# Attention planned by TensorE tiling, with the Newton step of the inverse roots on GpSimd

## The chip, the cores and the metric

The kernel runs on one core of a Trainium2 chip. The metric is the device time in microseconds (us) of one execution. The engines of the core run side by side and are synchronised by semaphores: TensorE (matrix products, in the profile PE, and PEld for its weight loads), VectorE (DVE), ScalarE (ACT), GpSimd (POOL), and SyncE (SP), from whose queue all DMA transfers are issued. SBUF is the working memory of 128 partitions, PSUM the memory of eight banks that TensorE writes to.

## The reference

Three parts follow one another: attention with normalised queries and keys, a soft mixture of experts, and a gated product.

```python
# q, k, v: batch 4, heads 12, seq 448, head_dim 64
def rmsnorm(x, g):
    rms = np.sqrt(np.mean(x * x, axis=-1, keepdims=True) + 1e-06)
    return x / rms * g
q_n, k_n = (rmsnorm(q, g_q), rmsnorm(k, g_k))
scores = scale * np.matmul(q_n, k_n.transpose(0, 1, 3, 2))
scores = scores - np.max(scores, axis=-1, keepdims=True)
attn = np.exp(scores)
attn = attn / (np.sum(attn, axis=-1, keepdims=True) + 1e-09)
attn_out = np.matmul(attn, v)
...
# x: 1792 x 768 from attn_out; phi: 768 x 32; w1, w2: 8 experts, 768 x 1024 and 1024 x 768
logits = x @ phi
# softmax over tokens picks slot inputs, each expert: relu(slots @ w1[e]) @ w2[e],
# softmax over slots mixes the expert outputs back to tokens
...
a = x @ w_a          # 768 x 1536
b = x @ w_b
return a * b @ w_out # 1536 x 768
```

## The kernel before, in words

Everything that the change touches lies in attention, the first of three stages in the program (some 340 us of the profiled execution). Attention works on 24 pairs of heads (`p`), each with two heads (`hd`) and four chunks of 112 rows (`c` for queries, `kc` for keys). For each pair the steps are:

- `LQ`, `LV`: loads of q, k and of v from DRAM (SP). Three pairs of q and k fit in SBUF (`qk`); the next load waits until `NM` has read an older one.
- `SQ`: squares of q (`i` = 0, GpSimd, except for the first three pairs) and of k (`i` = 1, ScalarE); `SS`: their sums over the head dimension (VectorE).
- `RT`, function `root`: the inverse roots on ScalarE as exp(-0.5 ln x), three instructions on 112 x 16 values. Two of them are the same exponential, one written to SBUF (`nt`) and one to PSUM.
- `NW`, function `newton`: one Newton step of the inverse roots, on VectorE, three instructions on 112 x 16 values. Its scratch is in PSUM, in the unused columns of the bank `psv` (`spare_ps`), whose other columns hold the value products `A`.
- `NM`: q and k times the roots (GpSimd; `i` = 0 on VectorE for two pairs). `T`: transposes on TensorE. `H` and `L`: each value is split into a high and a low part (ScalarE, VectorE); `Z`: six DMA transfers that stack these for the scores.
- `X`, function `peak`: products of the high parts, two matmuls side by side, one for each head, on 64 rows of the array each. `MX`: their maxima on VectorE. One PSUM buffer (`x`) serves all `X`. `R` and `RW`: the maxima as rows.
- `S`, function `score`: two matmuls for each chunk and head, on the full array (lines 346 and 347). `E`: the exponential (ScalarE).
- `AD`: additions of exponentials over the chunks (GpSimd). `A`, function `av`: the products with v, four matmul records, each head on 64 columns of the array. `D`, function `den`: the sums, likewise on 64 columns. `LN`, `EX`, `N1`, `N2`, `F`: reciprocals and the output of the pair.

After each six pairs the operations of the experts' softmaxes for that batch are mixed in (`moe_ops`): logits `lm` and `ln` and token sums `ac` are matmuls with 32 columns each, so on column strips.

The order of the instructions on each engine is made when the program is built, by a planner. `op` enters an operation with its engine, a cost, a due time (`prio`: the pair's number times `T0` = 11.5 plus the offset of its kind in `OFF`), its dependencies, and buffers that it takes and gives. `plan` then plays the operations through: each engine that is free takes, of the operations that are ready and have room, the one with the earliest due time. The instructions are written out in the order of the planned starts, and each engine runs its own in that order, waiting wherever its data isn't there. Where TensorE has a planned gap at the start or at the end of attention, matmuls on the identity fill it (`warm`), as do `W0` of them at the very start, in the bank `psv`.

Eight loads of expert weights, 1.5 MB each, are issued among the pairs' transfers; the other weights follow as the buffers of attention come free.

Of the kernel before, what the change touches and what calls it, by code (L numbers as in the profile page):

```python
# [32 lines left out]
def kernel(  # L33
# [20 lines left out]
    NC = 4  # L54
# [19 lines left out]
    W0 = 22  # L74
    SQ_ACT = (1,)
    NPT, T0, MSTEP, WU0, WUS, MF, = 5, 11.5, 3.2, 4, 2, 13
    OFF = dict(LQ=-29.0, LV=-12.6, SQ=14.4, SS=32.6, RT=21.7, NW=-22.2, NM=9.2, T=-16.7, H=-11.9, L=9.7, Z=5.9, X=-9.0, MX=-2.3, R=0.4, RW=13.2, S=5.4, E=8.3, AD=-29.5, A=19.0, D=7.6, LN=-51.5, EX=-19.7, N1=-7.9, N2=7.7, F=-53.1)
    MO = (-0.1, -0.9, 21.5, 82.1)
# [127 lines left out]
    with ExitStack() as c1:  # L206
# [52 lines left out]
        def root(p):  # L259
            t = sm.tile([P, 16], F32, tag="nt", name="nt", bufs=2)  # L260
            act.activation(out=t, in_=ssq_t[p].rearrange("p a c -> p (a c)"), func=AF.Ln, bias=ssq_eps[0:P])
            act.activation(out=spare_ps(0, 16), in_=t, func=AF.Exp, scale=-0.5)  # L262
            act.activation(out=t, in_=t, func=AF.Exp, scale=-0.5)
            nt_t[p] = t

        def newton(p, s):
            t, x, y = spare_ps(16, 16), ssq_t[p].rearrange("p a c -> p (a c)"), nt_t[p]
            if s == 0:
                dve.scalar_tensor_tensor(out=t, in0=spare_ps(0, 16), scalar=-0.5, in1=y, op0=ALU.mult, op1=ALU.mult)
            elif s == 1:  # L270
                dve.scalar_tensor_tensor(out=t, in0=x, scalar=D * 1e-6, in1=t, op0=ALU.add, op1=ALU.mult)
            else:
                r = rinv_t[p] = sm.tile([P, 2, 8], F32, tag="rinv", name=f"rinv{p}", bufs=3)
                dve.scalar_tensor_tensor(
                    out=r.rearrange("p a c -> p (a c)"), in0=t, scalar=1.5, in1=y, op0=ALU.add, op1=ALU.mult
                )
# [126 lines left out]
        def op(eng, cost, prio, name, fn, deps=(), take=(), give=()):  # L403
            names[name] = len(ops)
            ops.append((eng, cost, prio, fn, [names[d] for d in deps], take, [(k, names[n]) for k, n in give]))
            return name
# [4 lines left out]
        def pair_ops(p):  # L411
# [15 lines left out]
            for s in range(3):  # L427
                op("DVE", 0.20, o("NW"), ("NW", p, s), lambda s=s: newton(p, s), [("NW", p, s - 1) if s else ("RT", p)])
# [216 lines left out]
        def start_up():  # L645
            ps = ps_of["w"] = bank
            warm(ps, W0)

# [682 lines left out]
```

## Time and profile before

| | |
|---|---|
| median of 3 runs | 591.88 us (587.56, 591.88, 592.78) |
| profiled execution | 587.84 us, span 586.1 us |
| mean granted TensorE clock | 0.981 |
| TensorE busy | 557.8 us (95%), 3564 matmuls |
| VectorE busy | 333.9 us (57%) |
| ScalarE busy | 319.1 us (54%) |
| GpSimd busy | 231.4 us (39%) |
| mean DMA rate | 229 GB/s, 427 GB/s between 370 and 480 us |

The span is the time from the first to the last instruction of one profiled execution. A busy share is an average over all three stages. Matmuls are pipelined and their ends are modelled, so consecutive ones overlap in the records; what one takes is read from its start to the start of the next.

### The profile page before, as it was taken

The numbers are of one execution on the slowest core, as the hardware profiler recorded it, in microseconds if no ns is written. First come the engines' busy times: TensorE is split into PE (matmuls) and PEld (weight loads), VectorE is DVE, ScalarE is ACT, GpSimd is POOL, SyncE is SP. The second block draws the span as 40 slices with busy tenths as digits, with TensorE's granted clock in tenths as the row PEclk, the third lists the DMA queues.
The fourth block names the chain that finished last, engine by engine and source line by source line (L and its number), as shares of the span: only waits on it lengthen the run. The fifth ranks groups of instructions, "written<-read, shape, count | busy, mean of one in ns | idle before, by whom it ended". The sixth has DMA issues, their size and how long they took to land.

```text
span 586.1 us, 9656 instructions
## 1 busy us (share of the span) xinstructions
PE 557.8 (95%) x3564; PEld 326.8 (56%) x3564; DVE 333.9 (57%) x556; ACT 319.1 (54%) x607; POOL 231.4 (39%) x167
## 2 busy tenths in 40 slices
PE   8799999999999899999999999898999999999997
PEld 8645444444444444443454455333675656689996
DVE  2778778677776467877656331122248788742211
ACT  4367767667666457666666531111279889432210
POOL 1288887567785356886654700011100000200000
PEclk9999999999999599999999998999999999999999
DMA  6598699969899378999684869999999991002332
GB/s 164 131 232 188 154 271 265 203 192 214 240 202 259 67 211 180 260 211 249 141 218 111 326 244 410 427 427 423 423 425 423 421 426 57 0 29 83 98 89 81
DMA packets 42622, 134.42 MB, mean 229 GB/s; under 512 B 5840, under 2 KB 31440, under 8 KB 36176
## 3 DMA queue, kind: packets, MB, share of 16 engines
q1 hardware_dynamic: 42576, 133.81, 74.7%
q8 instruction: 28, 0.46, 0.3%
q14 instruction: 18, 0.15, 0.1%
HBM read 95.26 MB, written 5.51 MB: 172 GB/s over the span
## 4 chain that ended last, share of the span: by engine, by line
PE 81%; DMA 7%; DVE 5%; ACT 4%; issue 1%; POOL 1%; SPq 1%; ACTq 0%; DVEq 0%; POOLq 0%
PE psv L365 12%; PE pss L346 8%; PE pss L347 6%; PE psx L324 5%; DMA z<-e 4%; PE psM L1046 4%; PE psh L805 4%; PE psS L829 4%; PE pso L1246 3%; PE pso L1248 3%; PE pso L1247 3%; PE psden L373 3%; PE pst L293 3%; PE psv L201 3%; DMA xw<-in_k_dram 3%; PE psL L201 2%
## 5 line engine op out<-in xcount | busy, mean ns | idle before, releaser
L352 ACT ACTIVATE pt<-pss 112x448 f32<-112x448 f32 x192 | 98.2, 541 | 49.8 <-PE pss L347 44.1
L329 DVE TENSOR_REDUCE nmx<-psx 112x2 f32<-112x896 f32 x96 | 104.5, 1088 | 31.2 <-PE psx L324 30.1
L357 POOL TENSOR_TENSOR sum<-sum,pt 112x896 f32<-112x896 f32 x48 | 100.6, 2096 | 13.2 <-ACT pt L352 11.2
L365 PE MATMUL psv<-pt,v 112*64 112x448 f32 x384 | 94.2, 572 | 2.8 <-ACT psv L262 2.5
L346 PE MATMUL pss<-z 128*112 128x448 f32 x192 | 83.0, 432 | 1.0 <-DMA z<-e 0.9
L347 PE MATMUL pss<-z 66*112 66x448 f32 x192 | 71.6, 373 | 0.6 <-DMA z<-e 0.6
L281 POOL TENSOR_TENSOR n<-xw,rinv 112x512 f32<-112x512 f32 x46 | 48.3, 1064 | 60.4 <-PE pst L293 30.2
L357 POOL TENSOR_TENSOR sum<-pt,pt 112x896 f32<-112x896 f32 x24 | 50.3, 2096 | 32.7 <-ACT pt L352 24.2
L346 PEld LDWEIGHTS pss<-z 128*112 128x112 f32 x192 | 34.0, 177 | 42.8 <-issue 20.3
L324 PE MATMUL psx<-e 64*112 64x448 f32 x192 | 44.2, 456 | 1.9 <-DVE nmx L329 1.6
L324 PEld LDWEIGHTS psx<-e 64*112 64x112 f32 x192 | 16.7, 170 | 48.4 <-DVE nmx L329 16.1
L1246 PE MATMUL pso<-Mh,t 128*128 128x384 f32 x112 | 37.9, 339 | 0.5 <-DVE Ml L1075 0.5
L1248 PE MATMUL pso<-Mh,t 128*128 128x384 f32 x112 | 37.9, 338 | 0.0
L1247 PE MATMUL pso<-Ml,t 128*128 128x384 f32 x112 | 37.8, 338 | 0.0
L365 PEld LDWEIGHTS psv<-pt,v 112*64 112x64 f32 x384 | 19.7, 137 | 31.5 <-issue 22.2
L1098 POOL TENSOR_TENSOR t<-CC,t 128x512 fp32r<-128x512 f32 x2 | 3.7, 1882 | 82.0 <-DVE G L1005 82.0
L347 PEld LDWEIGHTS pss<-z 66*112 66x112 f32 x192 | 34.4, 179 | 2.8 <-DMA z<-e 1.1
L1265 DVE COPY ot<-pso 128x384 f32<-128x384 f32 (+1 forms) x14 | 7.6, 544 | 49.7 <-PE pso L1250 49.7
L1046 PE MATMUL psM<-w,G 128*128 128x512 f32 x64 | 33.8, 610 | 0.8 <-DVE G L1009 0.8
L255 DVE TENSOR_REDUCE ssq<-sq 112x8 f32<-112x512 f32 x48 | 31.9, 677 | 4.3 <-POOL sq L250 3.2
L908 ACT ACTIVATE top<-wu_w,few 128x1536 f32<-128x1536 int8 x18 | 31.4, 1746 | 0.4 <-DVE xw L926 0.4
L926 DVE SCALAR_TENSOR_TENSOR xw<-wu_w,top 128x768 int32<-128x768 int32 x24 | 22.2, 954 | 15.7 <-ACT top L912 15.7
(186 smaller groups left out, 966.3 us busy)
## 6 DMA issues: line engine op xcount, KB each, us to landing
wu_w<-in_moe_w_dram SPq DMA_DIRECT2D x38, 1536.0 KB, 13.3
z<-e SPq DMA_DIRECT2D x48, 336.0 KB, 5.7
z<-e SPq DMA_DIRECT2D x48, 224.0 KB, 6.1
r<-in_moe_w_dram SPq DMA_DIRECT2D x7, 1536.0 KB, 9.9
xw<-in_moe_w_dram SPq DMA_DIRECT2D x4, 1536.0 KB, 13.5
xw<-in_q_dram SPq DMA_DIRECT2D x24, 224.0 KB, 5.4
xw<-in_k_dram SPq DMA_DIRECT2D x24, 224.0 KB, 5.4
v<-in_v_dram SPq DMA_DIRECT2D x24, 224.0 KB, 4.4
```

What stands on the lines that cost most here:

```text
L281: eng.tensor_tensor(out=n_t[p][:, i].rearrange("p c h d -> p h c d"), in0=qk_t[p][:, i].rearrange("p h (c d) -> p h c d", d=D), in1=rinv_t ...
L324: pe.matmul(ps[:, hd], et[r, QH, c * P:(c + 1) * P], et[r, KH, :], start=True, stop=True)
L329: dve.tensor_reduce(out=nm_t[p][:, c, :], in_=ps_of[p, "x"], axis=AX.X, op=ALU.max, negate=True)
L346: pe.matmul(ps, z[:, 1, c], z[:, 0, :], start=True, stop=False)
L347: pe.matmul(ps, z[0:66, 2, c], z[0:66, 3, :], start=False, stop=True)
L352: act.activation(out=pt_t[p, kc][:, hd, :], in_=ps_of.pop((p, kc, hd)), func=AF.Exp)
L357: pool.tensor_tensor(out=sum_t[p], in0=pt_t[p, 0] if kc == 1 else sum_t[p], in1=pt_t[p, kc], op=ALU.add)
L365: pe.matmul(av_t[p][hd * D:(hd + 1) * D, 0:S], v_t[p][:, hd, kc, :], pt_t[p, kc][:, hd, :], start=(kc == 0), stop=(kc == NC - 1),)
L1046: pe.matmul(o, G[:, r], W[:, c], start=st, stop=sp_)
L1246: pe.matmul(o, ch[:, m], Mh[:, m, c], start=(m == 0), stop=False)
L1247: pe.matmul(o, ch[:, m], Ml[:, m, c], start=False, stop=False)
L1248: pe.matmul(o, cl[:, m], Mh[:, m, c], start=False, stop=False)
```

## The change

The planner learns of the way in which a matmul tiles TensorE's array. Each operation gets a mode (`MODES`): 0 full array, 1 row halves (`X`), 2 column halves (`A`, `D`), 3 column strips (`lm`, `ln`, `ac`). On TensorE the planner adds `MW` = 18.97 to the due time of an operation whose mode differs from that of the one before, when it chooses, and `MSW` = 0.1 us to its cost, when it is taken. The other TensorE costs are changed, and all offsets in `OFF` and `MO`.

The Newton step moves from VectorE (three operations of the plan) to GpSimd (one operation, four instructions), all of whose operands lie in SBUF. The root writes both its results to SBUF; its third instruction squares the second one's result.

At the start, `W0` falls from 22 to 8 identity matmuls; ahead of them stand 16 pairs of 448-column matmuls on `zt[1]` (`WR`), tiled in row halves, into the buffer of `X`. The operation `ones` on ScalarE, which now also fills `zt[1]`, is planned ahead of it.

```diff
--- before.py
+++ after.py
@@ -71,11 +71,12 @@
     LW, LO, LG = 8, 4, 2
     XLAST = 5
     NU = 3076
-    W0 = 22
+    W0, WR = 8, 16
     SQ_ACT = (1,)
     NPT, T0, MSTEP, WU0, WUS, MF, = 5, 11.5, 3.2, 4, 2, 13
-    OFF = dict(LQ=-29.0, LV=-12.6, SQ=14.4, SS=32.6, RT=21.7, NW=-22.2, NM=9.2, T=-16.7, H=-11.9, L=9.7, Z=5.9, X=-9.0, MX=-2.3, R=0.4, RW=13.2, S=5.4, E=8.3, AD=-29.5, A=19.0, D=7.6, LN=-51.5, EX=-19.7, N1=-7.9, N2=7.7, F=-53.1)
-    MO = (-0.1, -0.9, 21.5, 82.1)
+    OFF = dict(LQ=-166.2, LV=33.1, SQ=261.0, SS=546.8, RT=249.0, NW=-272.3, NM=304.6, T=-12.7, H=222.0, L=-181.2, Z=-53.0, X=-22.7, MX=346.8, R=1.6, RW=16.9, S=10.7, E=21.9, AD=-243.9, A=25.1, D=-215.8, LN=-88.7, EX=-311.9, N1=-104.9, N2=245.2, F=3.0)
+    MODES, MSW, MW = {"X": 1, "A": 2, "D": 2, "lm": 3, "ln": 3, "ac": 3}, 0.1, 18.97
+    MO = (28.8, 9.4, 27.9, 225.6)
     WE = 7
     WN = 11
     WS = 3
@@ -257,23 +258,20 @@
             )
 
         def root(p):
-            t = sm.tile([P, 16], F32, tag="nt", name="nt", bufs=2)
-            act.activation(out=t, in_=ssq_t[p].rearrange("p a c -> p (a c)"), func=AF.Ln, bias=ssq_eps[0:P])
-            act.activation(out=spare_ps(0, 16), in_=t, func=AF.Exp, scale=-0.5)
-            act.activation(out=t, in_=t, func=AF.Exp, scale=-0.5)
+            t = sm.tile([P, 2, 16], F32, tag="nt", name="nt", bufs=2)
+            act.activation(out=t[:, 0], in_=ssq_t[p].rearrange("p a c -> p (a c)"), func=AF.Ln, bias=ssq_eps[0:P])
+            act.activation(out=t[:, 0], in_=t[:, 0], func=AF.Exp, scale=-0.5)
+            act.activation(out=t[:, 1], in_=t[:, 0], func=AF.Square)
             nt_t[p] = t
 
-        def newton(p, s):
-            t, x, y = spare_ps(16, 16), ssq_t[p].rearrange("p a c -> p (a c)"), nt_t[p]
-            if s == 0:
-                dve.scalar_tensor_tensor(out=t, in0=spare_ps(0, 16), scalar=-0.5, in1=y, op0=ALU.mult, op1=ALU.mult)
-            elif s == 1:
-                dve.scalar_tensor_tensor(out=t, in0=x, scalar=D * 1e-6, in1=t, op0=ALU.add, op1=ALU.mult)
-            else:
-                r = rinv_t[p] = sm.tile([P, 2, 8], F32, tag="rinv", name=f"rinv{p}", bufs=3)
-                dve.scalar_tensor_tensor(
-                    out=r.rearrange("p a c -> p (a c)"), in0=t, scalar=1.5, in1=y, op0=ALU.add, op1=ALU.mult
-                )
+        def newton(p):
+            x, t = ssq_t[p].rearrange("p a c -> p (a c)"), nt_t[p]
+            r = rinv_t[p] = sm.tile([P, 2, 8], F32, tag="rinv", name=f"rinv{p}", bufs=3)
+            y = r.rearrange("p a c -> p (a c)")
+            pool.tensor_scalar(out=y, in0=x, scalar1=D * 1e-6, scalar2=None, op0=ALU.add)
+            pool.tensor_tensor(out=y, in0=y, in1=t[:, 1], op=ALU.mult)
+            pool.tensor_scalar(out=y, in0=y, scalar1=-0.5, scalar2=1.5, op0=ALU.mult, op1=ALU.add)
+            pool.tensor_tensor(out=y, in0=y, in1=t[:, 0], op=ALU.mult)
 
         def normalise(p, i, eng):
             if i == 0:
@@ -402,7 +400,8 @@
 
         def op(eng, cost, prio, name, fn, deps=(), take=(), give=()):
             names[name] = len(ops)
-            ops.append((eng, cost, prio, fn, [names[d] for d in deps], take, [(k, names[n]) for k, n in give]))
+            mode = MODES.get(name[1] if isinstance(name[0], int) else name[0], 0)
+            ops.append((eng, cost, prio, fn, [names[d] for d in deps], take, [(k, names[n]) for k, n in give], mode))
             return name
 
         def late_for(kind, at):
@@ -424,15 +423,14 @@
                    [("SQ", p, i)] + ([("SS", p, 0)] if i else []), (),
                    (("sq", ("SQ", p, i)),))
             op("ACT", 0.74, o("RT"), ("RT", p), lambda: root(p), [("SS", p, 0), ("SS", p, 1)])
-            for s in range(3):
-                op("DVE", 0.20, o("NW"), ("NW", p, s), lambda s=s: newton(p, s), [("NW", p, s - 1) if s else ("RT", p)])
+            op("Pool", 0.55, o("NW"), ("NW", p), lambda: newton(p), [("RT", p)])
             for i in range(2):
                 d = p < 2 and i == 0
                 op("DVE" if d else "Pool", 0.62 if d else 1.05, o("NM", i * 0.5), ("NM", p, i),
                    lambda i=i, d=d: normalise(p, i, dve if d else pool),
-                   [("NW", p, 2)] + ([("NM", p, 0)] if i else []), () if i else ("n",), (("qk", ("LQ", p)),) if i else ())
+                   [("NW", p)] + ([("NM", p, 0)] if i else []), () if i else ("n",), (("qk", ("LQ", p)),) if i else ())
             for i in range(2):
-                op("PE", 0.44, o("T", i * 2), ("T", p, i), lambda i=i: turn(p, i),
+                op("PE", 0.39, o("T", i * 2), ("T", p, i), lambda i=i: turn(p, i),
                    [("NM", p, i)] + ([("T", p, 0)] if i else []), ("m",) if i else ("m", "e"),
                    (("n", ("NM", p, 0)),) if i else ())
                 op("ACT", 0.62, o("H", i * 2), ("H", p, i), lambda i=i: high(p, i),
@@ -443,20 +441,20 @@
                 op("SP", 2.2, o("Z", hd), ("Z", p, hd), lambda hd=hd: stack(p, hd), [("L", p, 0), ("L", p, 1)] + ([("Z", p, 0)] if hd else []), () if hd else ("z",))
                 op(None, 4.0, 0, ("z", p, hd), None, [("Z", p, hd)])
             for c in range(NC):
-                op("PE", 0.26, o("X", c * 1.5), ("X", p, c), lambda c=c: peak(p, c),
+                op("PE", 0.285, o("X", c * 1.5), ("X", p, c), lambda c=c: peak(p, c),
                    [("H", p, 0), ("H", p, 1)] + ([("X", p, c - 1)] if c else []),
                    ("x",) if c else ("x", "nm"))
                 op("DVE", 1.09, o("MX", c * 1.5), ("MX", p, c), lambda c=c: peak_out(p, c), [("X", p, c)], (),
                    (("x", ("X", p, c)),))
             op(None, 0, 0, ("ef", p), None, [("X", p, NC - 1), ("z", p, 0), ("z", p, 1)], (),
                (("e", ("T", p, 0)),))
-            op("PE", 0.40, o("R"), ("R", p), lambda: rows(p), [("MX", p, c) for c in range(NC)] + [("Z", p, 0)], ("m",),
+            op("PE", 0.38, o("R"), ("R", p), lambda: rows(p), [("MX", p, c) for c in range(NC)] + [("Z", p, 0)], ("m",),
                (("nm", ("X", p, 0)),))
             op("ACT", 0.91, o("RW"), ("RW", p), lambda: rows_out(p), [("R", p), ("Z", p, 0)], (), (("m", ("R", p)),))
             for kc in range(NC):
                 for hd in range(2):
                     x = (2 * kc + hd) * T0 / 8
-                    op("PE", 0.44, o("S", x), ("S", p, kc, hd), lambda kc=kc, hd=hd: score(p, kc, hd),
+                    op("PE", 0.41, o("S", x), ("S", p, kc, hd), lambda kc=kc, hd=hd: score(p, kc, hd),
                        [("RW", p), ("z", p, hd)], ("s",), (("z", ("Z", p, 0)),) if (kc, hd) == (NC - 1, 1) else ())
                     op("ACT", 0.55, o("E", x), ("E", p, kc, hd), lambda kc=kc, hd=hd: expo(p, kc, hd),
                        [("S", p, kc, hd)] + ([("E", p, kc, 0)] if hd else []), () if hd else ("pt",),
@@ -465,12 +463,12 @@
                     op("Pool", 2.12, o("AD", kc * T0 / 4), ("AD", p, kc), lambda kc=kc: addup(p, kc),
                        [("E", p, kc, 1), ("E", p, kc - 1, 1)] + ([("AD", p, kc - 1)] if kc > 1 else []),
                        ("sum",) if kc == 1 else ())
-                op("PE", 0.94, o("A", kc * T0 / 4), ("A", p, kc), lambda kc=kc: av(p, kc),
+                op("PE", 0.81, o("A", kc * T0 / 4), ("A", p, kc), lambda kc=kc: av(p, kc),
                    [("E", p, kc, 1), ("lv", p)] + ([("A", p, kc - 1)] if kc else []), () if kc else ("vb",),
                    (("v", ("LV", p)),) if kc == NC - 1 else ())
                 for x in () if kc == 0 else (0, 1) if kc == 1 else (kc,):
                     op(None, 0, 0, ("pf", p, x), None, [("A", p, x), ("AD", p, max(x, 1))], (), (("pt", ("E", p, x, 0)),))
-            op("PE", 0.97, o("D"), ("D", p), lambda: den(p), [("AD", p, NC - 1)], ("m", "rd"),
+            op("PE", 0.81, o("D"), ("D", p), lambda: den(p), [("AD", p, NC - 1)], ("m", "rd"),
                (("sum", ("AD", p, 1)),))
             op("ACT", 0.64, o("LN"), ("LN", p), lambda: den_ln(p), [("D", p)])
             op("ACT", 0.58, o("EX"), ("EX", p), lambda: den_exp(p), [("LN", p)])
@@ -589,7 +587,7 @@
                 op(e, 0.5, t[0], n("xc", c, h), lambda: xt_copy(c, h), [n("xt", c, h)], (), (("m", n("xt", c, h)),))
 
             def acc_ops(h):
-                op("PE", 0.80, at(step), n("ac", h), lambda: accum(h), [n("ec")] + [n("xc", c, h) for c in range(NC)],
+                op("PE", 0.72, at(step), n("ac", h), lambda: accum(h), [n("ec")] + [n("xc", c, h) for c in range(NC)],
                    ("m",), [("xtok", n("xt", c, h)) for c in range(NC) if not (last and h)])
                 op("DVE", 0.61, t[0], n("ao", h), lambda: accum_out(h), [n("ac", h)], (), (("m", n("ac", h)),))
 
@@ -643,8 +641,14 @@
             return s
 
         def start_up():
-            ps = ps_of["w"] = bank
-            warm(ps, W0)
+            ps_of["w"] = bank
+            ps = ps_x.tile([128, 2, 512], F32, tag="x", name="psw")[0:P, :, 0:S]
+            for x in range(WR):
+                for hd in range(2):
+                    r = slice(hd * D, (hd + 1) * D)
+                    z = zt[1][r, 0, x % 2]
+                    pe.matmul(ps[:, hd], z[:, x % 4 * P:(x % 4 + 1) * P], z, start=True, stop=True)
+            warm(bank, W0)
 
         def load_g():
             for i, g in enumerate((g_q, g_k)):
@@ -657,14 +661,20 @@
             )
 
         def fill_ones():
+            for x in range(2):
+                act.activation(
+                    out=zt[1][:, 0, x].rearrange("p (c x) -> p c x", c=NC),
+                    in_=ident[:, 0:P].unsqueeze(1).to_broadcast([128, NC, P]), func=AF.Copy,
+                )
             for z in zt:
                 for hd in range(2):
                     act.activation(
                         out=z[64:66, hd, 2, :], in_=ident[64:66, 64 + hd:65 + hd].to_broadcast([2, S]), func=AF.Copy
                     )
 
-        op("PE", 3.0, -1e3, ("warm",), start_up, (), ("vb",))
-        op("ACT", 2.4, -1e3, ("ones",), fill_ones)
+        op("ACT", 3.5, -1e3, ("ones",), fill_ones)
+        op("PE", 4.0, -1e3, ("warm",), start_up, (), ("vb", "x"))
+        op(None, 0, 0, ("wx",), None, [("warm",)], (), (("x", ("warm",)),))
         pool.memset(ones, 1.0)
         pool.memset(eps, EPS)
         op("SP", 2.0, late_for("LQ", 0) + 2, ("lg",), load_g)
@@ -692,7 +702,7 @@
                 for d in o[4]:
                     users[d].append(i)
             at, start, end, free = [0.0] * len(ops), {}, {}, {}
-            ready, events = {}, [(0.0, -1)]
+            ready, events, mode = {}, [(0.0, -1)], 0
 
             def push(i):
                 bisect.insort(ready.setdefault(ops[i][0], []), (ops[i][2], i))
@@ -720,15 +730,25 @@
                     for eng, rd in list(ready.items()):
                         if eng and free.get(eng, 0) > t + 1e-9:
                             continue
-                        for x, (_, i) in enumerate(rd):
+                        x, best = None, 0.0
+                        for y, (prio, i) in enumerate(rd):
+                            if x is not None and prio >= best:
+                                break
                             if at[i] <= t + 1e-9 and room(ops[i][5]):
-                                break
-                        else:
+                                v = prio + (MW if eng == "PE" and ops[i][7] != mode else 0.0)
+                                if x is None or v < best:
+                                    x, best = y, v
+                                if eng != "PE":
+                                    break
+                        if x is None:
                             continue
-                        rd.pop(x)
+                        i = rd.pop(x)[1]
+                        more = 0.0
+                        if eng == "PE":
+                            more, mode = MSW if ops[i][7] != mode else 0.0, ops[i][7]
                         for k in ops[i][5]:
                             taken[k].append(i)
-                        start[i], end[i] = t, t + ops[i][1]
+                        start[i], end[i] = t, t + ops[i][1] + more
                         if eng:
                             free[eng] = end[i]
                         heapq.heappush(events, (end[i], i))
```

## Rows read from the trace of the kernel before

**Rows 1.** Busy time by stretch of the span: engine busy us, TensorE clock, DMA share, GB/s.

```profile
60.00:100.00 40.00, 39.25 (x193) 17.86 (x191) 31.97 (x55) 29.77 (x67) 33.02 (x22) 1.00 0.93 220
220.00:260.00 40.00, 40.00 (x204) 18.38 (x203) 29.93 (x46) 27.22 (x56) 30.81 (x21) 1.00 0.92 213
```

**Rows 2.** Timeline of TensorE, 232 to 235 us: start, us, line, operation.

```profile
232.17 0.46 PE L346 MATMUL pss<-z 128*112 128x448 f32 x1
232.47 0.37 PE L347 MATMUL pss<-z 66*112 66x448 f32 x1
232.67 0.36 PE L346 MATMUL pss<-z 128*112 128x448 f32 x1
232.87 0.37 PE L347 MATMUL pss<-z 66*112 66x448 f32 x1
233.17 0.97 PE L365 MATMUL psv<-pt,v 112*64 112x448 f32 x4
234.07 0.46 PE L324 MATMUL psx<-e 64*112 64x448 f32 x2
234.46 0.54 PE L552 MATMUL psx<-ident,xT 128*112 128x128 f32 x3
```

**Rows 3.** Timeline of TensorE, 49.5 to 51.2 us: two value products in a row.

```profile
49.54 1.72 PE L365 MATMUL psv<-pt,v 112*64 112x448 f32 x8
51.19 0.45 PE L346 MATMUL pss<-z 128*112 128x448 f32 x1
```

**Rows 4.** Timeline of TensorE: the first and the last value products of attention.

```profile
33.62 0.97 PE L365 MATMUL psv<-pt,v 112*64 112x448 f32 x4
...
336.96 1.67 PE L365 MATMUL psv<-pt,v 112*64 112x448 f32 x8
```

**Rows 5.** Timeline of all engines, 189 to 203 us; in brackets idle time and releaser.

```profile
189.01 1.04 POOL L250 TENSOR_TENSOR sq<-xw 112x512 f32<-112x512 f32 x1 [3.78 <-DMA xw<-in_q_dram]
...
192.31 1.76 PE L365 MATMUL psv<-pt,v 112*64 112x448 f32 x4 [2.53 <-ACT psv L262]
...
203.00 1.04 POOL L281 TENSOR_TENSOR n<-xw,rinv 112x512 f32<-112x512 f32 x1 [0.74 <-PE pst L293]
```

**Rows 6.** Busy time by stretch, 190 to 205 us, columns as in rows 1.

```profile
190.00:195.00 5.00, 2.69 (x8) 0.76 (x8) 3.00 (x7) 2.63 (x7) 2.09 (x2) 0.66 1.02 203
195.00:200.00 5.00, 5.00 (x18) 3.10 (x18) 3.37 (x6) 2.26 (x4) 0.00 (x0) 0.50 0.04 14
200.00:205.00 5.00, 5.00 (x14) 2.40 (x10) 0.94 (x4) 2.25 (x6) 3.73 (x3) 0.50 0.00 0
```

**Rows 7.** Groups by line, whole span: busy us, mean ns, idle before and releasers.

```profile
L329 DVE TENSOR_REDUCE nmx<-psx 112x2 f32<-112x896 f32 x96 | 104.5, 1088 | 31.2 <-PE psx L324 30.1
L299 ACT ACTIVATE e<-pst 128x448 fp32r<-128x448 f32 x24 | 13.0, 542 | 12.8 <-PE pst L293 10.3 <-DMA xw<-in_k_dram 1.7 <-DMA xw<-in_q_dram 0.5
```

**Rows 8.** Waits, who for whom: us in total, times, longest us.

```profile
DVE rinv L274 <- PE psv L365: 3.6, 4, 1.5
ACT psv L262 <- PE psv L201: 1.7, 1, 1.7
PE psx L324 <- DVE nmx L329: 1.6, 2, 1.4
```

**Rows 9.** The bank `psv` and its instructions: duration ns min/median/max, first and last start.

```profile
L269 DVE SCALAR_TENSOR_TENSOR psv<-psv,nt x24: 172/183/183, 10.0 to 283.2; 112x16 f32<-112x16 f32 x24
```

**Rows 10.** Groups by line on GpSimd: its smallest instructions.

```profile
L961 POOL COPY selab<-i 64x64 f32<-64x64 f32 x2 | 0.5, 232 | 0.1
...
L669 POOL MEMSET eps<- 128x1 f32 x1 | 0.1, 98 | 0.0
```

**Rows 11.** Waits of GpSimd for loads of q, columns as in rows 8.

```profile
POOL sq L250 <- DMA xw<-in_q_dram: 8.5, 5, 3.8
```

**Rows 12.** Timeline of SyncE's queue, 180 us: issue of a load of q.

```profile
180.03 0.32 SPq L236 DMA_DIRECT2D xw<-in_q_dram  x1
```

**Rows 13.** The page's DMA issues: count, KB each, median us from issue to landing.

```profile
xw<-in_q_dram SPq DMA_DIRECT2D x24, 224.0 KB, 5.4
```

**Rows 14.** Timeline of TensorE, start of the span: the warming matmuls.

```profile
1.42 7.97 PE L201 MATMUL psv<-ident 128*128 128x128 f32 x44 [1.42 <-POOL ident masks.py:199]
```

## The prediction

> **What bounds the kernel now.** First the page's engine totals (the table above): TensorE is busy 95%, the next engine 57%. Such a share is an average over stages, so I cut the span into stretches. Attention, which holds everything that the change touches, runs to about 340 us. In its steady stretches TensorE is busy 39 to 40 of 40 us at full clock, while VectorE, ScalarE and GpSimd are busy 27 to 33 [rows 1]. There a microsecond of TensorE's own work is worth a microsecond, and one of another engine nothing until TensorE waits for it. From about 325 us the expert weights stream in, as attention's buffers come free; if attention ends earlier, the stream begins earlier, so I carry gains over to the end one for one.
>
> Then the timeline of TensorE alone, read from start to start, because the busy times of matmuls overlap. A matmul of a score among scores takes 0.20 us to the next start. The first one after a value product takes 0.30, and so does the last one ahead of it; the value product itself (four matmuls) takes 0.90 [rows 2]. Set alone between scores it costs 0.90 + 0.10 + 0.10 = 1.10 us. Where two follow each other they take 1.65 together, so the second costs 0.75 [rows 3]. Two changes of tiling thus cost 1.10 - 0.75 = 0.35, or 0.17 us each. I counted the changes among full array, row halves (peaks), column halves (value products and sums) and column strips (logits, token sums) from 33 us, just ahead of the first value product, to the end of attention (first and last product: [rows 4]): 350 changes, with 141 runs of the full array, 89 of peaks, 110 of products or sums and 11 of strips. So 350 x 0.17 = 60 us of attention go into changes.
>
> Last, the waits. TensorE has few, but its largest is strange: the value product at 192.31 us sat 2.53 us for ScalarE's write of a root into the bank `psv` [rows 5]. Nothing in the product needs that root, which belongs to a pair whose load came late (its square waited 3.78 us); the two share one PSUM bank, and the wait follows the bank. Behind it the clock is at half until about 205 us [rows 6].
>
> **The change, part by part.**
>
> *Grouping.* The plan now adds 0.1 us for each change and takes an operation of the same tiling if its due time is within 18.97 of the best. What can it merge? Peaks have one buffer, and VectorE reads each for 1.09 us [rows 7], while its two matmuls take 0.39 [rows 2]; two can't follow each other, so 89 to 96 runs stay. Value products and sums can pair up, as there are five buffers of exponentials: 110 runs become 60 to 85. Today 70 of the 210 runs that aren't full-array follow one another directly. At the same share, 60 paired runs give 160 such runs, 107 full ones and 267 in all; 85 give 185, 123 and 308. I take 285, which is 65 fewer: 65 x 0.17 = **-11 us**. Bounds: 0 (nothing merges) and -17 (250 in all). Longer runs keep ScalarE waiting for scores; its idle quarter hides that [rows 1].
>
> *Newton out of the bank.* The root's first result and Newton's scratch leave PSUM, so the 2.53 us wait goes, and with it the slow clock behind it: 0.66 over 5 us is 3.4 us at half, and 0.50 over 10 us makes 13.4 us, with TensorE busy in most of it, so 6.7 us lost [rows 6]. Together **-9.2 us**. In a second place TensorE's peaks waited 1.4 us for VectorE's maxima, whose queue stood behind a Newton step that waited 1.5 us for a value product [rows 8]: **-1.4**. What is late next at 192 us? Not the root's own pair: GpSimd's next normalisation of any pair runs at 203.00 and then waits for a transpose, not for Newton [rows 5].
>
> *Newton on GpSimd.* VectorE loses three instructions of 0.18 us a pair [rows 9], 0.54 x 24 = 13 us, all in its idle quarter: 0. GpSimd gets four of 112 x 16 elements, which this trace doesn't show on it. Its nearest rows bound one: 0.098 us (memset of one column) and 0.23 (copy of 64 x 64) [rows 10], so 0.4 to 0.93 us a pair; the shape is nearer to the first, I take 0.6. GpSimd is busy 33 of 40 us in its fullest stretch [rows 1], which is some 3.1 pairs (24 pairs in 305 us, 12.7 each), so about 2.2 us a pair are free. Cost 0; with that cover gone, up to 0.93 x 24 = 22 us.
>
> The Trainium skill speaks against this move: "GPSIMD Engine Reference", Engine selection, sends elementwise work to VectorE and calls GpSimd about twice as slow with two inputs. By that ratio the two instructions with two tensor inputs would take 0.36 us and the others 0.18, an estimate of 1.08 us a pair, and the sum would stay, as the free time still covers it. No row here shows such a small one on both engines.
>
> Root keeps three ScalarE instructions, a square in place of an exponential: 0. But Newton now stands in GpSimd's queue, ahead of the additions of exponentials and of the next normalisation. A late root holds these, and behind them sums, buffers of exponentials and TensorE. That wait is new. GpSimd's queue already waited 8.5 us for late loads in five squares [rows 11]; I let some two thirds as much reach TensorE: **+6 us** (bounds 0 and +8.5).
>
> *Start-up.* Two copies of 128 x 448 at 0.54 us [rows 7] stand ahead of the first squares on ScalarE: 0 to +1.1 us. Of the warming, 14 plain matmuls go, each two records, at 7.97 us for 44 records 14 x 0.36 = 5.1 us; 16 pairs of 448 columns come, each between 0.20 (two such matmuls side by side, as one score matmul) and 0.78 (a peak's 0.39 at half clock), 3 to 12 us, I take 5; it can begin about 3 us instead of 1.42 [rows 14], after the copies. Against that, the first root's write no longer waits 1.7 us for warming matmuls in its bank [rows 8]. Net **-1 us**, bounds -4 and +8.
>
> *New due times.* All offsets are new, and many so large that a kind of work always comes first or last on its engine (sums of squares, maxima and normalisation last). The work is the same; its new order can't be read from this trace. The +6 stands for this too.
>
> **The sum.** Against the profiled execution of 587.84 us: -11 - 9.2 - 1.4 - 1 + 6 = -16.6, so 571. The median of the runs shown is 591.88, with 587.56 and 592.78 as ends; the profiled one is at the fast end. I add 2 us, half of that distance: **573 us**.
>
> **Rivals.**
> - *Grouping gives nothing.* The greedy choice finds no work of the same tiling ready, or longer runs starve ScalarE; only the bank counts: 573 + 11 = 584 us. For: peaks can't merge, and a third of the runs already meet. Against: products and sums can.
> - *The stall moves.* A late load stops GpSimd once as it stopped TensorE, and the 9.2 come back: 582 us. For: Newton in GpSimd's queue. Against: 2.2 us of slack a pair.
> - *Slower.* Eight weight loads of 1.5 MB go out during attention. In front of the stall, a load of q issued at 180.03 us was read only at 189.01 [rows 5, 12], where 5.4 us is the median landing [rows 13]. If such a load holds GpSimd at Newton, stops the additions and leaves TensorE idle for 2.5 us and then at half clock, each costs 9.2. With none the time is 573, with two 591 (no gain), from three on slower: 573 + 28 = 601. For: the plan counts 4.2 us for a load, weights or not. Against: today one of eight did it.
> - *More than forecast.* 250 changes (6 us more), no late waits (6), start-up at its best (3): 573 - 15 = 558.
>
> **How the numbers follow.** Forecast 0.55 (562 to 580), grouping void 0.15, stall moved 0.14, slower 0.09, more 0.07. Leaving out the slower case and the far side of the best gives 558 to 591. A measurement of this kernel tells about 1% from no change, 586 to 598. Faster: the 0.55, the 0.07, and of the two middle rivals 0.09 each, 0.80; same 0.11; slower 0.09.
>
> **What would show it.** Right: fewer than 310 changes of tiling in TensorE's timeline, more value products in sets of eight matmuls, no TensorE wait for the root, full clock from 40 to 330 us, four GpSimd instructions of 0.1 to 0.23 us a pair, attention over near 325 us. Wrong: as many changes as now (grouping void); GpSimd idle ahead of Newton or the additions, with TensorE idle soon after (stall moved, or slower); or TensorE waiting for maxima, which VectorE now takes last.

## The result, and the profile after

The changed kernel takes 569.64 us (median of 4 runs, 567.6 to 572.02), the one before 592.33 (587.56 to 597.49, beside it). The ratio is 0.9644, 95% interval 0.9568 to 0.972. (Ratios with an interval, here and below, leave out runs that a lower clock had slowed; medians take all runs.) The forecast was 573, with 558 to 591. The profiled execution went from 587.84 to 570.63 us.

Attention, in stretches as in [rows 1], and then cut into three parts for its granted clock, with the whole from the first to the last value product below:

```profile
60.00:100.00 40.00, 40.00 (x206) 20.42 (x205) 30.08 (x40) 30.34 (x64) 36.08 (x39) 1.00 0.90 234
...
220.00:260.00 40.00, 39.35 (x214) 20.57 (x213) 27.55 (x39) 28.55 (x60) 32.35 (x33) 1.00 0.84 232
```
```profile
24.00:100.00 76.00, 73.91 (x386) 37.89 (x385) 56.84 (x75) 56.86 (x121) 68.25 (x73) 1.00 0.90 225
100.00:200.00 100.00, 97.25 (x546) 50.99 (x545) 74.27 (x110) 71.20 (x154) 78.42 (x75) 1.00 0.93 228
200.00:313.31 113.31, 110.75 (x604) 55.79 (x606) 74.20 (x104) 75.56 (x156) 83.11 (x72) 1.00 0.83 229
30.11:313.31 283.20, 276.01 (x1495) 140.64 (x1498) 199.42 (x280) 199.17 (x421) 225.66 (x211) 1.00 0.88 227
```

TensorE is as full as before, and the half clock of [rows 6] is gone. The stretch from the first value product to the end of the last fell from 305.0 to 283.2 us. GpSimd is busier, 36 of 40 us at its fullest.

The end of attention in TensorE's and GpSimd's timelines, beside [rows 3, 4]:

```profile
310.08 3.23 PE L363 MATMUL psv<-pt,v 112*64 112x448 f32 x16
313.24 0.85 PE L569 MATMUL psacc<-xtok,etok 112*32 112x384 f32 x8
...
316.12 0.97 PE L371 MATMUL psden<-sum,ones 112*64 112x448 f32 x4
```
```profile
308.86 2.11 POOL L355 TENSOR_TENSOR sum<-pt,pt 112x896 f32<-112x896 f32 x1 [5.01 <-ACT pt L350]
311.05 4.26 POOL L355 TENSOR_TENSOR sum<-sum,pt 112x896 f32<-112x896 f32 x2
```

Four value products stand in one run here (16 records). Counted as in the prediction, attention has 253 changes of tiling where it had 350: the runs of products and sums went from 110 to 66, those of peaks stayed at 89. But TensorE ends its last product at 313.3 us, and the last sums (`psden`) come behind it, at 316.1: GpSimd's last addition ends at 315.3. From the last product to `psst`, the first matmul on the finished token sums, it is 330.28 - 313.31 = 17.0 us, where it was 350.99 - 338.63 = 12.4.

Waits of TensorE in attention, loads of q, and the Newton step on GpSimd:

```profile
PE psx L322 <- DVE nmx L327: 4.2, 8, 1.0
PE psv L363 <- DVE xT L393: 0.8, 1, 0.8
PE pst L291 <- POOL n L279: 0.6, 2, 0.4
```
```profile
xw<-in_q_dram SPq DMA_DIRECT2D x24, 224.0 KB, 4.3
```
```profile
L271 POOL TENSOR_SCALAR rinv<-ssq x24: 253/254/259, 7.5 to 270.3; 112x16 f32<-112x16 f32 x24
L272 POOL TENSOR_TENSOR rinv<-rinv,nt x24: 221/222/528, 8.4 to 271.2; 112x16 f32<-112x16 f32 x24
L273 POOL TENSOR_SCALAR rinv<-rinv x24: 204/204/206, 8.7 to 271.5; 112x16 f32<-112x16 f32 x24
L274 POOL TENSOR_TENSOR rinv<-rinv,nt x24: 221/222/225, 9.0 to 271.8; 112x16 f32<-112x16 f32 x24
```

No wait for a DMA, a root or a Newton step is left on TensorE, and none is longer than 1.0 us [rows 5, 8]; the waits for maxima grew from 1.6 to 4.2 us. Loads of q land in 4.3 us where they took 5.4 [rows 13]. The four GpSimd instructions take 254, 222, 204 and 222 ns by the medians, 0.90 us a pair.

### The profile page after: what moved, and what is told of

Read it like the earlier page. It is cut to its first block, busy times and chain, and to the rows that moved or that the text cites. A ratio compares the mean times of both kernels' runs of the same rounds, so it can differ in the third digit from the quotient of the medians.

```text
span 568.8 us, 9655 instructions
## 1 busy us (share of the span) xinstructions
PE 541.6 (95%) x3576; PEld 330.8 (58%) x3576; DVE 323.1 (57%) x484; ACT 319.9 (56%) x609; POOL 252.3 (44%) x263
## 4 chain that ended last, share of the span: by engine, by line
PE 72%; POOL 8%; DVE 7%; issue 4%; ACT 4%; DMA 1%; SPq 1%; ACTq 0%; POOLq 0%; DVEq 0%
PE psv L363 10%; PE pss L344 6%; POOL sum L355 5%; PE pss L345 5%; PE psh L825 5%; PE psM L1066 4%; PE psx L322 4%; PE psS L849 4%; PE pso L1266 4%; PE pso L1268 3%; PE pso L1267 3%; PE psden L371 3%; PE pst L291 3%; PE psL L202 2%; PE psS L1066 2%
## 5 line engine op out<-in xcount | busy, mean ns | idle before, releaser
L350 ACT ACTIVATE pt<-pss 112x448 f32<-112x448 f32 x192 | 94.9, 543 | 21.0 <-PE pss L345 16.5
L363 PE MATMUL psv<-pt,v 112*64 112x448 f32 x384 | 84.7, 552 | 1.0 <-DVE xT L393 0.8
L344 PE MATMUL pss<-z 128*112 128x448 f32 x192 | 79.1, 412 | 0.0
L363 PEld LDWEIGHTS psv<-pt,v 112*64 112x64 f32 x384 | 23.1, 136 | 35.2 <-issue 30.2
L256 DVE TENSOR_REDUCE ssq<-sq 112x8 f32<-112x512 f32 x48 | 32.2, 679 | 19.8 <-POOL sq L251 18.2
L946 DVE SCALAR_TENSOR_TENSOR xw<-wu_w,top 128x768 int32<-128x768 int32 x24 | 22.2, 953 | 17.3 <-ACT top L932 17.3
```

Source lines behind the costliest of these rows:

```text
L344: pe.matmul(ps, z[:, 1, c], z[:, 0, :], start=True, stop=False)
L350: act.activation(out=pt_t[p, kc][:, hd, :], in_=ps_of.pop((p, kc, hd)), func=AF.Exp)
L363: pe.matmul(av_t[p][hd * D:(hd + 1) * D, 0:S], v_t[p][:, hd, kc, :], pt_t[p, kc][:, hd, :], start=(kc == 0), stop=(kc == NC - 1),)
```

## The experiments

**How the times are read.** Runs of one kernel differ by up to 5% (before: 580.36 to 610.35 us in 28 runs), and the mean granted clock of the run moves with them: 0.995 at 580.36, 0.944 at 610.35. Time times clock is nearly constant: 577.5 and 576.2. So beside the median I give this product, an estimate of the time at full clock: it holds the order of work and its waits, and what the median adds to it is taken as lost at half clock. The changes of tiling are counted in the traces; the expectations count them in the plan, one or two apart.

| kernel | median us | time x clock, median (range) | changes |
|---|---|---|---|
| before (28 runs) | 591.1 | 576.9 (575.1 to 581.2) | 350 |
| changed (4) | 569.6 | 563.2 (562.6 to 564.1) | 253 |
| changed, second set (4) | 568.3 | 563.2 (561.8 to 564.1) | 253 |
| before + Newton on GpSimd | 584.1 | 570.8 (569.7 to 573.3) | 342 |
| before + grouping | 598.1 | 585.5 (584.5 to 587.8) | 241 |
| before + new due times | 572.6 | 568.3 (567.6 to 568.6) | 322 |
| changed, old due times | 610.5 | 583.0 (581.4 to 583.8) | 235 |
| changed, no preference | 573.7 | 569.1 (568.6 to 570.3) | 328 |
| changed, Newton as before | 571.0 | 565.0 (563.6 to 566.4) | 240 |
| changed, old start | 569.1 | 562.9 (562.9 to 563.9) | 253 |
| changed, Newton on VectorE in SBUF | 591.8 | 572.5 (571.2 to 576.1) | 235 |
| changed, Newton's planned cost 0.92 | 578.7 | 567.2 (565.2 to 568.8) | 232 |
| changed, last sums on VectorE (8 runs) | 567.2 | 561.0 and 560.5 (560.1 to 562.0) | 252 |

**One part alone: the Newton step.** The diff's hunks for `root`, `newton` and their entry in the plan, on the kernel before.

> The kernel before, with root and Newton step as in the changed kernel (operands in SBUF, GpSimd), old offsets, old plan. Its TensorE order holds 341 changes of tiling against 350. Theory (a change costs 0.17 us, the shared bank costs 10.6 us): 9 x 0.17 = 1.5 and 10.6 less, 580 us, no TensorE wait for the root. Rival (the stall moves to GpSimd's queue): 590 us or more, with GpSimd waiting ahead of the Newton step. Rival (new due times did it all): 590, too, but without that wait.

584.1 us, where the kernel before took 594.2 beside it, with single runs from 572.4 (clock 0.996) to 605.45 (0.941); ratio 0.9738 (0.9568 to 0.9908). By the product it is 6.1 us. The profiled execution is the one of 605.45 us. No wait for the bank is left in it, but TensorE waits three times for the stacked operands of the scores (0.9, 2.4 and 2.5 us), and over the 11, 32 and 22 us from 37, 88 and 279 us the clock is 0.53, 0.52 and 0.53:

```profile
PE pss L343 <- DMA z<-e: 5.8, 3, 2.5
```
```profile
88.00:120.00 32.00, 31.99 (x91) 13.11 (x92) 14.30 (x19) 14.57 (x30) 14.19 (x16) 0.52 0.78 178
```

So under the old due times the bank was one of several late things. The first theory's size (12 us) comes near in the medians (10), with runs 33 us apart. Of the 6 us by the product 4.1 are there before the first value product, which starts at 29.48 us where it was 33.62 [rows 4].

**One part alone: grouping.** The planner's modes and new TensorE costs on the kernel before; everything else old.

```diff
+    MODES, MSW, MW = {"X": 1, "A": 2, "D": 2, "lm": 3, "ln": 3, "ac": 3}, 0.1, 18.97
...
+                                v = prio + (MW if eng == "PE" and ops[i][7] != mode else 0.0)
```

> The kernel before with only the planner's modes and new TensorE costs; Newton in the bank on VectorE, old offsets, old start. 243 changes in TensorE's order against 350. Theory: 107 x 0.17 = 18 us less, 574 us, with waits for the bank still in the trace. Rival (grouping gives nothing without due times made for it, since longer runs starve the other engines): 590.

598.1 us, ratio 1.0156 (1.0019 to 1.0293): slower by some 1.6%, though 109 changes are gone, and 8.6 us more by the product. First to last product before and here, and the two longest waits here:

```profile
33.62:338.63 305.01, 298.26 (x1510) 138.59 (x1510) 211.37 (x344) 202.31 (x426) 211.47 (x133) 0.98 0.84 210
34.11:344.53 310.42, 288.06 (x1525) 145.39 (x1526) 211.52 (x346) 198.85 (x428) 212.19 (x133) 0.98 0.79 205
```
```profile
PE psx L325 <- DVE nmx L330: 8.0, 12, 1.5
PE psv L366 <- ACT psv L263: 3.0, 7, 0.6
```

TensorE is busy 288 us, 10 less than before in that stretch (298.3), but idle 22 instead of 7: its own work shrank, and waits took more than that, for maxima above all (8.0 us, 1.6 before [rows 8]). My step "-11 us for grouping" fails as an independent term; the rival (590) was the better description for the old due times, and even it was too low.

**All but the due times.** The changed kernel with the old `OFF` and `MO`.

> The changed kernel with the old offsets: modes, Newton on GpSimd and the new start stay. 235 changes. Theory (grouping and bank do it, due times little): 115 x 0.17 + 10.6 + 1 less than before, 561 us, no slower than the changed kernel's 570. Rival (the new due times are what pays): 580 to 590.

610.5 us, ratio 1.0314 (1.0194 to 1.0434): the worst of all, 20 us above the changed kernel by the product and 41 by the medians, and above the rival's range too. From the first product to the last:

```profile
32.91:370.16 337.25, 305.82 (x1503) 157.95 (x1503) 201.14 (x279) 201.13 (x419) 225.26 (x210) 0.90 0.75 190
```

TensorE is idle 31 of 337 us, and the clock is 0.90. My theory falls: without the new due times the other parts lose, 6 us by the product against the kernel before.

**The due times alone.** The kernel before with the new `OFF` and `MO`, nothing else.

```diff
-    OFF = dict(LQ=-29.0, LV=-12.6, SQ=14.4, SS=32.6, RT=21.7, ...
+    OFF = dict(LQ=-166.2, LV=33.1, SQ=261.0, SS=546.8, RT=249.0, ...
```

> The kernel before with nothing but the new offsets (due times) of all kinds; no modes, old TensorE costs, Newton in the bank on VectorE, old start. 321 changes of tiling against 350. New theory (the new due times keep loads and stacked scores ahead, so no long TensorE wait drops the clock): 578 to 582, full clock throughout. Theory of the prediction (due times alone give nothing but the fewer changes, 29 x 0.17): 587. Rival (they only fit the new costs): 595 or more.

572.6 us, ratio 0.9804 (0.9705 to 0.9903), or 18.5 us by the medians: most of the whole gain, from the part that I had booked as +6, and below the range of the new theory. The stretch, and its waits, with Newton still in the shared bank:

```profile
33.30:322.78 289.48, 285.75 (x1505) 135.12 (x1504) 211.70 (x342) 203.41 (x423) 210.94 (x132) 1.00 0.86 220
```
```profile
PE psv L201 <- ACT psv L262: 1.3, 1, 1.3
PE psv L365 <- DVE psv L271: 0.9, 1, 0.9
PE psx L324 <- DVE nmx L329: 0.9, 1, 0.9
PE psv L365 <- DVE rinv L274: 0.8, 1, 0.8
```
```profile
POOL sq L250 <- DMA xw<-in_q_dram: 1.0, 1, 1.0
```

The stretch lost 305.0 - 289.5 = 15.5 us. TensorE is busy 12.5 us less and idle 3.0 us less (3.7 for 6.8). Of the busy time some 6.7 us were half clock [rows 6], and 28 fewer changes make 28 x 0.17 = 4.8; 1 us stays open. The loads of q that GpSimd waits for cost 1.0 us, not 8.5 [rows 11]; TensorE waits 0.9 us at most for the bank from 40 us on, not 2.53; and the clock is full. So the two late things of [rows 5] do not meet in this trace.

**Grouping taken out.** The changed kernel with the preference at zero: `MW` = 0.0.

> The changed kernel with the preference for the same tiling at 0 instead of 18.97; the plan still adds 0.1 us for each change. 328 changes against 255. Theory: 73 x 0.17 = 12.4 us more than the changed kernel, 582 us. Rival (the changes cost nothing on the path, the other engines bound): 570.

573.7 us: 4 us above the changed kernel by the medians, 5.9 by the product. 328 changes instead of 253.

```profile
29.78:323.25 293.47, 289.27 (x1510) 135.25 (x1510) 199.78 (x281) 205.89 (x425) 227.75 (x211) 1.00 0.84 219
```

First to last product takes 293.5 us against 283.2, so grouping did save 10.3 us there. TensorE's busy time is 276.0 us with it and 289.3 without: its own work shrank by 13.3 us, 13.3 / 75 = 0.18 us a change, and its idle time grew from 4.2 to 7.2. The price was right (0.17). What grouping gained was given back: 4.6 us between the last product and `psst` (12.4 us here, 17.0 in the changed kernel), where GpSimd's additions end last. The profiled executions differ by another 2.6 us after the experts' start (235.0 and 232.4), but that is one execution's clock: the changed kernel profiled again takes 232.2 there.

**Newton as before.** The changed kernel with `root` and `newton` of before: scratch in the bank, VectorE. The scratch is a single buffer, and in its trace two roots are written (40.46 and 41.13 us) before the first Newton step reads (41.48), so one pair computes with another pair's root; the instructions are the same.

> The changed kernel with root and Newton step as before: scratch in the bank of the value products, Newton on VectorE in three instructions; modes, new due times and new start stay. 242 changes of tiling. Theory of the prediction (the shared bank costs some 10 us): 579 us, TensorE waiting for the root or the Newton step. New theory (the bank cost that much only because its one long wait dropped TensorE's clock; with the new due times no long wait arises): 570 to 573, short waits for the bank, clock full.

571.0 us, 1.4 above (1.8 by the product). From 25 us on, the waits for the bank and TensorE's longest wait, and at the start the first root and the first value product:

```profile
PE psv L366 <- ACT psv L263: 2.0, 5, 0.6
PE psv L366 <- DVE rinv L275: 1.5, 3, 0.8
```
```profile
240.66 0.97 PE L374 MATMUL psden<-sum,ones 112*64 112x448 f32 x4 [2.83 <-POOL sum L358]
```
```profile
10.49 0.19 ACT L263 ACTIVATE psv<-nt 112x16 f32<-112x16 f32 x1 [2.78 <-PE psv L202]
...
34.46 0.97 PE L366 MATMUL psv<-pt,v 112*64 112x448 f32 x4
```

No wait for the bank is over 0.8 us and the clock is full through attention, as the new theory has it; with the new due times leaving the bank is worth 1 to 2 us, not 10.6. Two things go beyond the theory. A long wait did arise, 2.83 us for GpSimd's sums, and the clock stayed at 1.00 from 238 to 243 us: what decides whether a wait drops it isn't shown. And the 1 to 2 us are a difference. The first root waits 2.78 us for the warming matmuls in its bank, and the first value product starts 4.4 us later than in the changed kernel; the stretch behind it is 1.8 us shorter (281.4 for 283.2), with 13 fewer changes.

**Newton on VectorE, in SBUF.** Three instructions, no PSUM.

```diff
+            dve.scalar_tensor_tensor(out=y, in0=x, scalar=D * 1e-6, in1=t[:, 1], op0=ALU.add, op1=ALU.mult)
+            dve.tensor_scalar(out=y, in0=y, scalar1=-0.5, scalar2=1.5, op0=ALU.mult, op1=ALU.add)
+            dve.tensor_tensor(out=y, in0=y, in1=t[:, 0], op=ALU.mult)
```

> The changed kernel with the Newton step on VectorE, three instructions, all operands in SBUF. 237 changes. If leaving the bank is what counts, and not the engine: as the changed kernel, 567 to 572. If VectorE's relief counts (maxima come last on it, and TensorE waits for them): 575 or more, with more waits of the peaks for maxima than the 4.7 us of the changed kernel.

591.8 us, ratio 1.0091 (1.0017 to 1.0166). The second theory's signs came (over 575 us, 14.7 us of waits of the peaks for maxima), but not by its cause: it is not that VectorE has three more instructions, the instructions themselves grew.

```profile
147.60 2.09 POOL L354 TENSOR_TENSOR sum<-sum,pt 112x896 f32<-112x896 f32 x1
147.71 2.02 DVE L273 TENSOR_TENSOR rinv<-rinv,nt 112x16 f32<-112x16 f32 x1
...
151.31 0.71 PE L321 MATMUL psx<-e 64*112 64x448 f32 x2 [2.60 <-DVE nmx L326]
```
```profile
L271 DVE SCALAR_TENSOR_TENSOR rinv<-ssq,nt x24: 164/460/1833, 8.2 to 276.2; 112x16 f32<-112x16 f32 x24
L272 DVE TENSOR_SCALAR rinv<-rinv x24: 174/175/2077, 8.5 to 277.0; 112x16 f32<-112x16 f32 x24
L273 DVE TENSOR_TENSOR rinv<-rinv,nt x24: 174/176/2084, 8.7 to 277.2; 112x16 f32<-112x16 f32 x24
```

Sixteen columns take 0.17 us alone and up to 2.08 beside an addition on GpSimd, and end when that ends (149.73 and 149.69 us). Of the 72 instructions 33 took more than 0.25 us, and each of these ended 0.03 to 0.04 us after a GpSimd instruction with two tensor inputs (an addition, a square or a normalisation). VectorE is busy 240 us in the stretch, where Newton with an operand in PSUM left it at 206; behind it wait the maxima, and TensorE for them: 2.60 us here. So the scratch in PSUM had a use: with one operand there, none of the 72 took over 0.18 us (Newton as before).

**A cost that changes no work.** The changed kernel with Newton's planned cost at 0.92 instead of 0.55.

> The changed kernel with nothing but the planned cost of the Newton step at 0.92 us, which is what its four GpSimd instructions take, in place of 0.55. The work is the same; only the order that the planner finds differs (234 changes of tiling against 255). Theory (the due times fit one plan of one set of costs, and any other order is worse by several us): 575 to 590. Rival (due times are good in themselves, and fewer changes help): 566 to 570.

578.7 us, ratio 0.988 (0.9781 to 0.9979). With 21 fewer changes, and with a cost nearer to the truth, it is 9 to 10 us slower (4 by the product). What happened at its worst place:

```profile
97.47 1.07 SPq L144 DMA_DIRECT2D wu_w<-in_moe_w_dram  x1
98.58 0.44 SPq L243 DMA_DIRECT2D v<-in_v_dram  x1
...
108.51 2.33 PE L363 MATMUL psv<-pt,v 112*64 112x448 f32 x6 [3.28 <-DMA v<-in_v_dram]
```
```profile
108.00:113.00 5.00, 4.49 (x14) 1.35 (x14) 0.00 (x0) 0.81 (x2) 0.22 (x1) 0.66 1.09 209
```

A load of v fell in just behind a weight load and landed 9.9 us after its issue, TensorE waited 3.28 us, and the clock dropped to 0.66 over the next 5 us. The due times fit one order; a nudge gives another, good or bad by several us. That limits what the part-by-part runs can say: each of them but the old start is also another order.

**The old start.** 22 identity matmuls, no fills; TensorE's order behind it is that of the changed kernel.

> The changed kernel with the start of before: 22 identity matmuls, no matmuls on the filled tile, no two fills on ScalarE. Behind the start TensorE's order is that of the changed kernel (255 changes). Prediction's step (start-up worth about 1 us, bounds -4 to +8): 570 to 572. Rival (the new start is what makes the first scores 2.3 us earlier): 572 to 573.

569.1 us beside 568.3 for the changed kernel on the same chip; 562.9 and 563.2 by the product. The new warming is worth nothing that shows, and the rival falls: the first value product comes at 29.39 us with the old start, so its early place (30.11 in the changed kernel, 33.62 before) is not the warming's doing.

**The end of attention.** The last pair's three additions on VectorE.

```diff
-            pool.tensor_tensor(
+            (dve if p == NPAIR - 1 else pool).tensor_tensor(
```

> The changed kernel with the three additions of exponentials of the very last pair on VectorE (planned 1.05 us each) in place of GpSimd (2.1 us each). Theory (GpSimd's additions are what the end of attention now waits for: its last one ended at 315.3 us, TensorE's last value product at 313.3): the last sums come 3 us earlier, 566 to 567 us. Rival (the weights' transfers bound what follows, whenever attention ends): 569 to 570.

> The changed kernel itself, beside the others on one chip: 568 to 572 us.

> The kernel of e10 once more (the last pair's additions of exponentials on VectorE), beside the changed kernel on the same chip. If the end of attention waits for GpSimd: 2 to 4 us below the changed kernel in the same call. Rival (chance): within 1 us of it.

567.0 us, and 567.4 beside 568.3 for the changed kernel on one chip. In the traces the theory holds: the sums' matmul comes at 312.77 us (317.23 in the changed kernel profiled beside it), and `psst` at 327.92 (331.39):

```profile
308.79 1.09 DVE L355 TENSOR_TENSOR sum<-pt,pt 112x896 f32<-112x896 f32 x1 [0.31 <-ACT pt L350]
310.33 2.28 DVE L355 TENSOR_TENSOR sum<-sum,pt 112x896 f32<-112x896 f32 x2
...
327.92 1.30 PE L815 MATMUL psst<-wsel,acc 128*128 128x32 f32 x10 [1.30 <-DVE wsel L811]
```

The profiled spans are 563.1 and 566.5 us, and the product is 2.7 lower, with every run below every run of the changed kernel. The medians, 0.9 apart, lie inside the rival's 1 us: by them it is no faster.

## Why the prediction was right, point by point

The time came within 4 us of the forecast, but its terms did not come as booked; errors cancelled.

- *What bounds the kernel*: right. TensorE sets attention, and attention's gain reaches the end nearly whole (`psh`, the first expert matmul, came 20.3 us earlier, the end of the span 17.3; in the second profile of the changed kernel 19.8 and 19.6).
- *Grouping, -11*: the count within its bounds but 97 fewer for 65, with 28 of them by the new due times alone; the price right (0.18 for 0.17). A step that failed is "there a microsecond of TensorE's own work is worth a microsecond": at the end of attention GpSimd's additions were next. Of the 10.3 us that the preference saves in the stretch, 4 to 6 are left. The Trainium skill, "TensorEngine Tiling (Array Packing)", Key Properties, says that a change of mode drains TensorE; the price measured here agrees with it.
- *Newton out of the bank, -9.2 and -1.4*: the mechanism was read rightly, and alone it gives 6 us by the product, 4 of them at the start. But the stall needed both the shared bank and a late load, and the new due times removed the load; together the bank is worth 1 to 2 us in all, less than the 4 by the product that a mere reordering moves. I priced one cause where two were needed. The -1.4 did not come: the waits for maxima, a sign that I had listed against me, rose to 4.2 us.
- *Newton on GpSimd, 0*: right, at the upper bound (0.90 us a pair for 0.6, bounds 0.4 to 0.93); some 57 us of the 283 were left idle. "GPSIMD Engine Reference" of the Trainium skill, Engine selection, spoke against it. The trace does not bear its ratio of two out at this size: 0.22 us on GpSimd against VectorE's 0.18 with an operand in PSUM, and up to 2.08 on VectorE all in SBUF. The same page's Specifications, that VectorE instructions with two SBUF inputs contend with GpSimd, agrees with those 2.02 us beside 2.09; I had not weighed it.
- *New due times, +6 with the new wait*: the step that failed most. Alone they measure -8.6 us by the product and -18.5 by the medians; taken out of the changed kernel they cost 19.8 by the product. I took "can't be read from this trace" for a cost, when the trace showed what due times could remove: 8.5 us of waits for loads, a 2.53 us stall and 6.7 us of half clock.
- *Start-up, -1*: too small, and its cause was the bank. The warming shows no difference. But the first peaks start at 16.1 to 17.6 us in every trace without scratch in the bank, and at 18.3 to 20.0 in those with it, and the first value product came 3.5 us earlier. I had the first root's wait for the warming matmuls [rows 8] as 1.7 us and did not follow it to the first product.
- *The late load on GpSimd's queue* (rivals two and three): GpSimd still waits 3.4 us for loads of q in the changed kernel (8.5 before [rows 11]), and none of it reaches TensorE as a wait over 1.0 us. A weight load that delays a pair's load does cost what the third rival says, a wait and then half clock, as the run with Newton's cost at 0.92 shows.

From 576.9 to 563.2 by the product is 13.7 us of better order; the other 9 us of the medians' 22.7 are half clock that the changed kernel falls into less (no longer in attention, still behind it). That split is worked out, not measured by itself. The two profiled executions place it: up to `psst` the changed kernel is 20.7 us ahead. Its first product comes 3.5 us earlier. Up to the last product TensorE is busy 22.3 us less, of which some 6.7 are half clock [rows 6] and 15.6 go with 97 fewer changes, 0.16 each. It is idle 0.4 us more: the 2.53 us stall went, waits for maxima came. And the end takes 4.6 us more. So the -9.2 came about as booked, grouping and start gave more, the +6 did not come, and the end was not booked at all.

## What to carry to other kernels

Before pricing a stall, ask what has to coincide for it: if two parts of a change each remove one of the causes, it must be counted once. Where an order is made by a planner, an experiment on one part is also another order, so measure how much a meaningless nudge moves (9 us here, 4 at full clock) before reading smaller differences. When the bounding engine gets faster, look at the last microseconds of the stage: here GpSimd, busy 77 to 83% before [rows 1], became what the end waits for.

## What the runs showed of the hardware that I had not expected

- A VectorE instruction of 16 columns with all operands in SBUF took up to 2.08 us beside a 2.09 us addition on GpSimd, and 0.18 at most with an operand in PSUM (72 of each); each of the 33 slow ones ended with a GpSimd instruction of two tensor inputs.
- The spread of a kernel's runs goes with TensorE's granted clock: 580.36 us at 0.995, 610.35 at 0.944, with the product within 1% of 577.
- A TensorE wait of 2.4 to 3.3 us was followed by half clock in three kernels, but one of 2.83 us in a fourth left the clock full.
